# A wave's attention moved behind its casts, wider fillers, and scores of two pairs in one stretch, in a fused attention and MLP kernel

## Chip, cores and metric

The kernel runs on one core of a Trainium2 chip. The metric is the device time of one execution in microseconds. Before the change it is 228.59 us (median of three executions, 228.53 to 228.61). An execution over 1.5% longer than the fastest of its kernel counts as slow. Ratios here use the other, fast, executions alone; the medians given beside them take in all executions of a run. The word "wave" below means 128 positions of each of four batches (512 rows); there are six waves, and in each wave the eight heads are taken as four pairs.

## The reference

```python
def _attn_ref(q, k, v, lam):           # blocks of 64, state carried on
    for b in range(nb):
        intra = (qb @ kb.T) * Dmask            # decay lam**(i-j), causal
        intra = intra @ vb
        inter = (qb * lam_pow) @ kv_state
        out[:, :, sl] = intra + inter
        kv_state = lam_block * kv_state + (kb * rev_pow).T @ vb
def _moe_ref(x, w_in, w_out):          # x: 3072 x 512, d_ff 2048
    h = x @ w_in
    return (h * sigmoid(1.702 * h)) @ w_out
```

The output of the attention, 3072 rows by 512, is the input of the MLP. The kernel uses blocks of 128, and works in bf16 with sums in fp32.

## The kernel before

Every pair p of a wave w passes through these steps. `S` is the scores, `sm` their masking on VectorE, `KV` the new state, `C` the output of the attention. All PSUM tiles below are one bank each: one for transposes, two for scores, one for KV, one for C, three for the MLP.

```python
def cast_k(w, p): ...   # VectorE from wave 2 on: bf16, scaled by the decay; waits for k's DMA
def cast_q(w, p): ...   # the same for q; from wave 2 on followed by a DMA transpose on the sync queue
def step_s(w, p):
    s2 = [ps.tile([P, B, P], f32, tag="s", bufs=2, name="ps_s") for _ in range(2)]
    for b in range(B):
        for h in range(2):               # 64 rows of the array for each head: half-array matmuls
            hs = slice(64 * h, 64 * h + 64)
            nc.tensor.matmul(s2[h][:, b, :], kq[hs, 0, b, :], kq[hs, 1, b, :], start=True, stop=True)
    for h in range(2):
        nc.vector.scalar_tensor_tensor(sm, s2[h], inv_pow[...], mask..., op0=MUL, op1=MUL)
def step_kv(w, p):
    ps_kv = ps.tile([P, B, P], f32, tag="kv", name="ps_kv")     # 4 matmuls, then VectorE adds to kv_sb
def step_c(w, p):
    ps_o = ps.tile([P, B, P], f32, tag="o", name="ps_o")        # 12 matmuls, then ScalarE copies to xT
```

The order of the program is fixed by hand. `main` lists the MLP as items of four matmuls with 512 columns (35 items in waves 0 and 1, about 32 later); `side` puts the attention of the next wave, its casts and its loads between them. `n` is the index of a wave's first item, `e` that behind its last.

```python
for p in range(NP):
    side += [(n + 1 + 2.0 * p, (do_cast, w + 1, p))]
    if w == 1 and p < 2:
        side += [(n + 1 + 2.0 * p, (load, 2, [p + 2]))]
side += [(e - 18 + 2.1 * i, s) for i, s in enumerate(attn_steps(w + 1))]   # S+KV of pair p, then C of pair p-1
```

## Time and profile before

| | before |
|---|---|
| time, median of 3 | 228.59 us |
| time and span of the profiled execution | 226.78 us, 225.1 us |
| PE busy | 211.1 us (94%) |
| PE idle, 73.0 to 77.7 us | 3.95 of 4.7 us |
| one steady wave (wave 2's MLP to wave 3's) | 32.95 us |

The reader should note the second row now. The execution that left the trace was 1.8 us faster than the median. The prediction takes no account of this difference, and that is where it fails.

In a timeline, the first number is the start in us, the second the length; `x8` merges eight instructions, and brackets give how long the engine was idle before and who released it. The lines of the trace that carry the argument stand in the prediction.

### The profile page before, as it was taken

What the parts mean: (1) busy time and instruction counts of PE and PEld (TensorE: products, weight loads), DVE (VectorE), ACT (ScalarE), POOL (GpSimd) and SP (SyncE); (2) the same over time, 40 slices, a digit from 0 to 9 for tenths busy, and PEclk for the clock granted to TensorE, in tenths of its full rate; (3) what the DMA queues carried; (4) which work ended last, traced back from release to release, by engine and by line L of the source; (5) the groups of instructions that cost most, each with busy time, mean ns of one, the idle gap of its engine ahead of it and who ended that gap; (6) DMA issues with size and microseconds to landing.
All of it is one profiled execution on the core that took longest, in us unless ns stands there. A gap on an engine that the chain in (4) does not pass through costs nothing.

```text
span 225.1 us, 3897 instructions
## 1 busy us (share of the span) xinstructions
PE 211.1 (94%) x1514; PEld 112.9 (50%) x1514; DVE 89.8 (40%) x193; ACT 89.7 (40%) x160; POOL 31.8 (14%) x65
## 2 busy tenths in 40 slices
PE   7677999999999299999999999999999999999994
PEld 7565344466444145544455544455544555444454
DVE  0756000189623836280466180665270534100121
ACT  5665863265566011256511266411176321376100
POOL 7117900324021111200111000121000000000000
PEclk9999999999999889999999999999999999999999
DMA  6999999999999998949997159995173011200112
GB/s 129 221 200 219 201 192 205 217 213 275 201 218 197 202 227 191 257 107 159 227 221 177 47 136 191 200 225 142 47 162 71 3 47 47 96 0 0 43 50 96
DMA packets 101590, 34.08 MB, mean 151 GB/s; under 512 B 93636, under 2 KB 98628, under 8 KB 101572
## 3 DMA queue, kind: packets, MB, share of 16 engines
q1 hardware_dynamic: 97204, 29.90, 61.4%
q0 software_dynamic: 4224, 3.93, 11.0%
q8 instruction: 12, 0.20, 0.4%
q14 instruction: 6, 0.05, 0.1%
q10 hardware_dynamic: 144, 0.00, 0.0%
HBM read 27.27 MB, written 6.29 MB: 149 GB/s over the span
## 4 chain that ended last, share of the span: by engine, by line
PE 82%; SPq 6%; DVE 5%; DMA 4%; issue 1%; ACT 1%; DVEq 0%; ACTq 0%
PE ps_h L269 35%; PE ps_out L294 35%; SPq L89 6%; PE ps_o L256 4%; DVE sm L222 3%; PE ps_s L219 2%; PE ps_kv L232 2%; DMA vf<-in_v_dram 2%; PE ps_o L254 2%; PE ps_out L281 2%; DMA qf<-in_q_dram 1%; ACT g_sb L272 1%; DVE kv_151 L239 0%; DVE kv_153 L239 0%; DVE kv_152 L239 0%
## 5 line engine op out<-in xcount | busy, mean ns | idle before, releaser
L272 ACT ACTIVATE g_sb<-ps_h 128x512 bf16<-128x512 f32 x96 | 56.9, 597 | 36.8 <-PE ps_h L269 36.5
L294 PEld LDWEIGHTS <-g_sb 128*128 128x128 bf16 x368 | 34.7, 99 | 37.2 <-issue 1.6
L222 DVE SCALAR_TENSOR_TENSOR sm<-ps_s,inv_pow,mask 128x512 bf16<-128x512 f32 x48 | 33.8, 746 | 31.7 <-PE ps_s L219 31.5
L298 DVE COPY o_sb<-ps_out 128x512 f32<-128x512 f32 x21 | 14.5, 691 | 77.8 <-PE ps_out L294 77.7
L259 ACT CAST xT<-ps_o 128x512 bf16<-128x512 f32 x24 | 14.0, 584 | 64.6 <-PE ps_o L256 64.6
L294 PE MATMUL ps_out<-w_out_165,g_sb 128*128 128x512 bf16 x92 | 24.2, 390 | 0.0
L294 PE MATMUL ps_out<-w_out_166,g_sb 128*128 128x512 bf16 x92 | 23.6, 383 | 0.0
L294 PE MATMUL ps_out<-w_out_167,g_sb 128*128 128x512 bf16 x92 | 23.5, 379 | 0.0
L294 PE MATMUL ps_out<-w_out_164,g_sb 128*128 128x512 bf16 x92 | 23.3, 379 | 0.0
L269 PE MATMUL ps_h<-xT,w_in_163 128*128 128x512 bf16 x96 | 22.4, 379 | 0.0
L269 PE MATMUL ps_h<-xT,w_in_162 128*128 128x512 bf16 x96 | 21.7, 379 | 0.0
L269 PE MATMUL ps_h<-xT,w_in_161 128*128 128x512 bf16 x96 | 21.7, 379 | 0.0
L171 DVE TENSOR_SCALAR kqs<-kf,k_pow 128x256 bf16<-128x256 f32 x40 | 12.7, 348 | 14.8 <-DMA kf<-in_k_dram 9.3
L269 PEld LDWEIGHTS <-w_in_162 128*128 128x128 bf16 x96 | 9.4, 98 | 11.3
L269 PEld LDWEIGHTS <-w_in_161 128*128 128x128 bf16 x96 | 9.4, 98 | 11.3
L269 PEld LDWEIGHTS <-w_in_163 128*128 128x128 bf16 x96 | 9.2, 98 | 10.5
L269 PE MATMUL ps_h<-xT,w_in_160 128*128 128x512 bf16 x48 | 12.0, 379 | 0.7 <-ACT g_sb L272 0.7
L171 DVE TENSOR_SCALAR kqs<-qf,q_pow 128x256 bf16<-128x256 f32 x33 | 10.5, 348 | 3.6 <-DMA qf<-in_q_dram 3.6
L269 PE MATMUL ps_h<-xT,w_in_159 128*128 128x512 bf16 x48 | 11.7, 379 | 0.0
L307 PE MATMUL ps_warm<-ident 128*128 128x128 bf16 x106 | 9.3, 252 | 1.5 <-POOL ident masks.py:199 1.5
L219 PE MATMUL ps_s<-kqT 64*128 64x128 bf16 x128 | 6.6, 219 | 3.4 <-DVE sm L222 3.4
L219 PEld LDWEIGHTS <-kqT 64*128 64x128 bf16 x128 | 3.8, 94 | 10.2 <-issue 7.7
(132 smaller groups left out, 184.5 us busy)
## 6 DMA issues: line engine op xcount, KB each, us to landing
kf<-in_k_dram SPq DMA_DIRECT2D x48, 128.0 KB, 3.6
qf<-in_q_dram SPq DMA_DIRECT2D x48, 128.0 KB, 3.7
vf<-in_v_dram SPq DMA_DIRECT2D x48, 128.0 KB, 3.6
out_dram<-o_sb SPq DMA_DIRECT2D x23, 256.0 KB, 2.4
w_first<-in_moe_w_in_dram SPq DMA_DIRECT2D x1, 512.0 KB, 4.4
w_in_161<-in_moe_w_in_dram POOLq DMA_DIRECT2D x1, 512.0 KB, 6.5
w_in_162<-in_moe_w_in_dram POOLq DMA_DIRECT2D x1, 512.0 KB, 6.8
w_in_163<-in_moe_w_in_dram POOLq DMA_DIRECT2D x1, 512.0 KB, 8.6
```

Source lines behind the costliest of these rows:

```text
L89: nc.sync.dma_start(out=x[:, :, h, :], in_=src[:, 2 * p + h, w * P : (w + 1) * P, :].rearrange("b s d -> s b d"))
L171: eng.tensor_scalar(x[:, i, :, h, :], f[:, :, h, :], scalar1=pw[:, hd : hd + 1], scalar2=None, op0=MUL)
L219: nc.tensor.matmul(s2[h][:, b, :], kq[hs, 0, b, :], kq[hs, 1, b, :], start=True, stop=True)
L222: nc.vector.scalar_tensor_tensor(sm, s2[h], inv_pow[:, 2 * p + h : 2 * p + h + 1], mask.to_broadcast([P, B, P]), op0=MUL, op1=MUL)
L232: nc.tensor.matmul(ps_kv[:, b, :], ks[:, b, :], vt[:, b, 0:3:2, :], start=True, stop=True)
L256: nc.tensor.matmul(ps_o[:, b, :], vt[:, b, h : h + 2, :].rearrange("p c d -> p (c d)"), masked[w, p, h][:, b, :], start=(not w and h == 0) ...
L259: nc.scalar.copy(x, ps_o.rearrange("p b s -> p (b s)"))
L269: nc.tensor.matmul(h_ps[fc], w_in_sb[j][:, kc, i * P : (i + 1) * P], xT[w, kc], start=(kc == 0), stop=(kc == KC - 1))
L272: nc.scalar.activation(g_of[w][:, fc, :], h_ps.pop(fc), GELU)
L294: nc.tensor.matmul(ps_out, g_of[w][:, fc, g * P : (g + 1) * P], w_out_sb[j][:, fc % CW, :], start=(fc == 0), stop=(fc == FFC - 1))
L298: (nc.scalar.copy if w == 0 and g % 2 else nc.vector.tensor_copy)(o, ps_out)
L307: nc.tensor.matmul(warm_ps[:, 0, :], ident, ident, start=True, stop=True)
```

## The change

The masking of wave 2's scores stands behind casts that wait for DMA, and the next scores need the banks that it empties. The change moves wave 2's attention four items later and so lets PE do MLP work first. From wave 2 on, the scores of two pairs follow each other (one entry into the half array in place of two), for which the score banks become four, in one ring with the transposes and, in waves 0 and 1, KV. From wave 2 on KV shares the bank of C. C goes ahead of KV. Fillers that keep PE's clock up in the start-up get 512 columns, four times as wide.

```diff
-        ps_t = ps.tile([P, 2, B, P], bf16, tag="t", name="ps_t")
+        ps_t = ps.tile([P, 2, B, P], bf16, tag="s", bufs=4, name="ps_t")
+    def step_s2(w, p):
+        step_s(w, p)
+        step_s(w, p + 1)
-        s2 = [ps.tile([P, B, P], f32, tag="s", bufs=2, name="ps_s") for _ in range(2)]
+        s2 = [ps.tile([P, B, P], f32, tag="s", bufs=4, name="ps_s") for _ in range(2)]
-            ps_kv = ps.tile([P, B, P], f32, tag="kv", name="ps_kv")
+            ps_kv = ps.tile([P, B, P], f32, name="ps_kv", **(dict(tag="s", bufs=4) if w < 2 else dict(tag="o")))
...
-            nc.tensor.matmul(warm_ps[:, 0, :], ident, ident, start=True, stop=True)
+            nc.tensor.matmul(warm_ps, ident, ident.rearrange("p (o s) -> p o s", o=1).to_broadcast([P, B, P]),
+                             start=True, stop=True)
...
+        if w == 2:
+            at = (0, 1.7, 3.2, 4.8, 6.3, 7.2, 9, 10.4, 12, 13.5)
+        else:
+            at = (0, 2, 4, 6.5, 8.5, 10, 12, 14, 16.5, 18.5)
+        steps = [(f, w, p) for q in (0, 2) for f, p in ((step_s2, q), (step_c, q), (step_kv, q), (step_c, q + 1),
+                                                       (step_kv, q + 1))]
+        return [(i - (14 if w == 2 else 20), x) for i, x in zip(at, steps)]
...   (start-up: keep_warm(40) -> keep_warm(10), 8 and 10 -> 2, C ahead of KV, last KV of waves 0 and 1 later)
-                    side += [(e - 18 + 2.1 * i, s) for i, s in enumerate(attn_steps(w + 1))]
+                    side += [(e + i, s) for i, s in attn_steps(w + 1)]
```

## The prediction

> **What bounds the kernel now.** I read the page first, then the stages, then the order of time around the one bad stage. The page's summary of the engines says that TensorE (PE) is busy 94% of the 225.1 us span, and its row of 40 slices shows where the rest is:
>
> ```profile
> PE   7677999999999299999999999999999999999994
> ...
> PEclk9999999999999889999999999999999999999999
> ...
> DMA  6999999999999998949997159995173011200112
> ```
>
> The reader is to see three things. The first four slices (to about 22 us) are start-up. One slice in the middle (number 14, 73 to 79 us) is nearly empty, and the granted clock drops in it. DMA is full from the start until about there and loose afterwards. The busy time by stage puts numbers on it (columns: stretch and its length in us, then busy us of PE, PEld, DVE, ACT and POOL with instruction counts, granted clock, DMA share, GB/s):
>
> ```profile
> 58.50:73.00 14.50, 14.25 (x78) 6.37 (x75) 4.93 (x14) 9.92 (x17) 1.84 (x3) 1.00 1.04 203
> 73.00:77.70 4.70, 0.75 (x10) 0.43 (x10) 3.64 (x9) 0.00 (x0) 0.61 (x1) 0.93 1.09 213
> 77.70:96.20 18.50, 18.50 (x136) 9.95 (x137) 8.77 (x15) 2.34 (x4) 2.45 (x4) 0.92 0.93 215
> 96.20:129.20 33.00, 33.00 (x226) 16.70 (x225) 16.16 (x36) 11.89 (x20) 2.45 (x4) 1.00 0.82 160
> ```
>
> From 96.2 us on a wave is pure PE: 33 us of 33. So there only PE work can be saved. From 73.0 to 77.7 PE does 0.75 us of work in 4.7. The timeline of that stretch names the cause:
>
> ```profile
> 69.83 0.40 PE L219 MATMUL ps_s<-kqT 64*128 64x128 bf16 x8
> ...
> 74.87 0.35 DVE L171 TENSOR_SCALAR kqs<-qf,q_pow 128x256 bf16<-128x256 f32 x1 [0.20 <-DMA qf<-in_q_dram]
> 75.25 1.41 DVE L222 SCALAR_TENSOR_TENSOR sm<-ps_s,inv_pow,mask 128x512 bf16<-128x512 f32 x2
> 76.05 0.21 PE L219 MATMUL ps_s<-kqT 64*128 64x128 bf16 x1 [2.91 <-DVE sm L222]
> ...
> 77.69 0.58 PE L232 MATMUL ps_kv<-v_sb_144,kqs 128*128 128x128 bf16 x4 [0.59 <-DVE kv_155 L239]
> ...
> 78.07 1.91 PE L294 MATMUL ps_out<-w_out_165,g_sb 128*128 128x512 bf16 x4
> ```
>
> The scores of wave 2, pair 0, are done at 70.2 us. Their masking (sm) starts only at 75.25, because all of wave 2's casts stand ahead of it in VectorE's program, and the last ones wait for q's DMA. The two score banks stay full, so the scores of pair 1 hold PE up. After the gap the clock is down: the eight MLP matmuls from 78.07 to 80.8 take 2.9 us, where eight take 1.73 elsewhere.
>
> **What the Trainium skill says.** "TensorE: Matmul & The Clock Gate", Engine queue depths, calls VectorE a strict FIFO; the masking of finished scores behind a waiting cast agrees. The same page, HAM oscillation, says an idle gap over some 3.4 us lowers the clock; here the waits of 2.9, 0.45 and 0.6 us between 73.2 and 77.7 gave 0.92 to 0.93. "TensorEngine Tiling (Array Packing)", Key Properties, says that changing the tiling mode drains PE. I work this out from the trace: the last MLP matmul before a score stretch ends at 83.39 (four at 215.7 ns from 82.52), scores start at 83.48, and the next full-array matmul at 83.81. Eight score matmuls, two at a time, need about 0.22 us of array time, and took 0.42; so about 0.2 us per stretch is entering and leaving.
>
> **The change, part by part.**
>
> *Start-up.* 40 fillers of 128 columns took 4.25 us (106 ns each, half rate); 10 of 512 are the same columns, so the same time. Later groups go from 8 or 10 small ones (0.45 to 0.56 us) to 2 large ones (about 0.43), and 12 ahead of the first MLP matmuls vanish; KV of the last two pairs also moves out of the way. I estimate 0.3 us at the first MLP matmul and up to 0.7 us more at the first gelus (the ACT copies of KV, 0.76 us, leave their path). I count **0** of it in the total: DMA runs at 190 to 240 GB/s in every stage up to 77.7 us, the sync queue issues without a pause from 35.8 to 76.5 us, and what it loads sets the end of wave 2's casts (75.2 us) whatever PE does earlier. PE only arrives earlier and waits longer.
>
> *Wave 1.* The one ring of four score banks takes A, S, S, KV per pair, just what the separate banks 1+2+1 allowed: 0.
>
> *Wave 2.* The first scores move from 18 to 14 items before the end of wave 1's MLP list. An item is four 512-column matmuls, 0.863 us. In the new order (read from the built program) PE does 2 more mlp1 items and 2 mlp2 items first, then all 16 scores of pairs 0 and 1 into four free banks, then 2 items, then C of pair 0. Without an upstream gain the scores start at 69.83 + 3.45 = 73.28, and the two items end at 73.28 + 0.64 + 1.73 = 75.65. C of pair 0 needs sm, which still ends at 76.66 (75.25 + 1.41, DMA-gated). In wave 1 C ends 0.60 us after its last sm (57.70 to 58.30), so C0 ends at 77.26: about 1 us of waiting in place of 4 us, and no drop of the clock.
>
> From there I add durations of this trace: item 0.863, C 0.667 (12 matmuls at 55.6 ns), KV 0.22, double scores 0.64. KV and C now share the one "o" bank. The KV update on VectorE starts 0.52 us after KV's first matmul (48.73 to 49.25) and takes 0.97, and PE resumes about 0.13 later (77.54 to 77.69): 1.62 us from KV's start to the next C. Where only one item stands between (0.22 + 0.86 = 1.08), that is a stall of **0.54 us**.
> - items 23, 24 to 78.99; KV0; item 25 to 80.07; stall to 80.61; C1 to 81.28
> - items 26, 27 to 83.00; KV1; item 28 to 84.09; scores of pairs 2, 3 to 84.73
> - sm of pair 2 ends at 84.18 + 0.43 + 1.41 = 86.02 to 86.03; item 29 ends at 85.6, so C2 ends at 86.63 and not 86.27: a stall of 0.36
> - items 30, 31 to 88.36; KV2; item 32 to 89.44; stall to 89.98; C3 to 90.65
> - items 33, 34 to 92.37; KV3; mlp1 of wave 2 starts at **92.6**.
>
> Before, it starts at 96.21. Gain **3.6 us**, after 1.44 us of new stalls.
>
> *Waves 3 to 5.* Two score stretches fewer per wave, each worth about 0.2 us: 0.4 a wave, **1.2 us**. Here two or three items stand between KV and C, and 1.73 us of items between the second score pair and C, so I expect no stall. Scores need pair 1's transpose earlier (12 items, 10.4 us after the wave's first mlp1). In the trace transposes start some 2.1 us after that point, 1.3 us apart, and land 3.3 us after issue: about 7 us. It fits.
>
> *The end* (last mlp2 pieces and the output) is untouched. Sum: 3.6 + 1.2 = 4.8 us; 228.6 - 4.8 = **223.7 us**.
>
> **The rivals.**
>
> *The shared bank bites harder.* KV and C alternate in one bank, evacuated by two engines. If each of the handovers in wave 2 costs a further 0.3 us, or some appear in waves 3 to 5, the time is 225 to 226. For it: VectorE is strictly in order, so a copy or an sm ahead of the KV update lengthens it. Against: after 78 us VectorE is busy less than half of the time (8.77 of 18.50).
>
> *The stalls are smaller than I add.* If VectorE picks KV up sooner, up to 1.4 us come back: 222.3. My latencies come from rows in which VectorE was free, so I hold most of this unlikely.
>
> *The start-up gain reaches the end.* It would add 0.5 to 1 us: 222.9. This needs DMA to come earlier, and nothing in its order changes.
>
> *DMA takes over.* If the transfers of wave 2 end at 75.2 and those of wave 3 matter next, wave 3 could stall, since PE arrives 3.6 us earlier. Its loads are issued from 76.6 to 91.3 us and take 3.6 us to land, its casts now start at about 93.5 us with pair 0, and pair 3's cast at 98.7: it fits, with little to spare for pair 0's output and transposes. Failing here would cost 1 to 2 us: 225.
>
> **Range and chances.** The gain in wave 2 is sure in sign: a 4.7 us hole is mostly filled with work that is there. Its size hangs on DMA's gate (half a us either way) and the stalls (0 to 2.5 us). The score saving is small but repeated. So 222.0 to 225.5 holds it 8 times in 10. The border of 2% is 224.02, only 0.3 us above my value: faster 0.62, within 2% 0.37, slower 0.01.
>
> **What would show each step.** Right: the slice at 73 to 79 us fills, with a granted clock near 1 in it; sm of wave 2's first pairs still starts near 75.2 us; first mlp1 of wave 2 near 92.6; steady waves of about 32.5 us (before: 32.9); short PE waits on the KV update before C of pairs 1 and 3 in wave 2, about 0.5 us each. Wrong: sm of wave 2 starting a us or more earlier or later (DMA moved with PE), PE waits ahead of C in waves 3 to 5, PE waiting on transposes, or a steady wave that is no shorter, which would mean that entering and leaving the half array is not what the 0.2 us were. Start-up may show mlp1 starting 0.3 us sooner, and wave 1 giving it back.

## The result, and the profile after

After: **221.61 us** (median of 4 executions, 221.56 to 221.85). Before, with one more execution: 228.56 us. The ratio is 0.9706, 95% interval 0.9683 to 0.9729. A ratio is the mean time of one kernel's fast executions over that of the other's from the same rounds, so it isn't quite the ratio of the medians. The result lies 2.1 us under my 223.7 and 0.4 under the end of my range.

The spans of the two profiled executions tell another story: 225.1 and 220.1 us, 5.0 us apart, where I had 4.8. The page of after has no row for the clock, as it never dropped. Its row of PE in 40 slices has lost the empty slice:

```profile
PE   7786999998999799999999999999999999999994
```

The stages of after, with the columns of the table in the prediction:

```profile
73.00:77.70 4.70, 3.35 (x37) 1.99 (x36) 2.90 (x6) 0.00 (x0) 0.62 (x1) 1.00 1.00 153
77.70:96.20 18.50, 17.90 (x133) 9.41 (x132) 11.65 (x23) 4.14 (x7) 2.47 (x4) 1.00 1.05 231
96.20:129.20 33.00, 33.00 (x228) 17.04 (x227) 17.78 (x43) 12.37 (x21) 2.46 (x4) 1.00 0.75 164
```

PE works 3.35 us of 4.7 where it worked 0.75, at a clock of 1.00. The timeline of after in wave 2:

```profile
72.90 0.62 PE L224 MATMUL ps_s<-kqT 64*128 64x128 bf16 x16
...
75.51 2.73 DVE L227 SCALAR_TENSOR_TENSOR sm<-ps_s,inv_pow,mask 128x512 bf16<-128x512 f32 x4
...
76.31 0.22 PE L257 MATMUL ps_o<-sm,v_sb_143 128*128 128x128 bf16 x1 [0.90 <-DVE sm L227]
...
76.97 0.22 PE L257 MATMUL ps_o<-sm,v_sb_143 128*128 128x128 bf16 x1 [0.44 <-DVE sm L227]
...
80.71 0.23 PE L255 MATMUL ps_o<-kqT,kv_152 128*128 128x128 bf16 x1 [0.20 <-DVE kv_155 L244]
...
86.19 0.22 PE L257 MATMUL ps_o<-sm,v_sb_145 128*128 128x128 bf16 x1 [0.19 <-DVE sm L227]
...
92.56 1.89 PE L270 MATMUL ps_h<-xT,w_in_159 128*128 128x512 bf16 x8
```

All 16 score matmuls of two pairs go out at once. The masking starts at 75.51, still behind the casts; PE waits 0.9 and 0.44 us in C of pair 0. Before C of pair 1 there is the wait for the KV update in the shared bank. The MLP of wave 2 starts at 92.56 us; the prediction has 92.6. The next wave's starts at 125.08, so a steady wave takes 32.52; the prediction has 32.5. These steps hold, and the total does not. The experiments had to find where two more microseconds come from.

### The profile page after: what moved, and what is told of

The parts are those of the page before. It is cut to its first block, busy times and chain, and to the rows that moved or that the text cites. A ratio compares the mean times of both kernels' runs of the same rounds, so it can differ in the third digit from the quotient of the medians.

```text
span 220.1 us, 3721 instructions
## 1 busy us (share of the span) xinstructions
PE 208.8 (95%) x1430; PEld 107.5 (49%) x1430; DVE 90.2 (41%) x193; ACT 89.3 (41%) x160; POOL 31.9 (14%) x65
## 4 chain that ended last, share of the span: by engine, by line
PE 58%; DVE 0%; issue 0%
PE ps_h L270 25%; PE ps_out L295 24%; PE ps_o L257 3%; PE ps_out L282 2%; PE ps_s L224 2%; PE ps_o L255 1%; PE ps_kv L237 1%; DVE o_sb L284 0%
## 5 line engine op out<-in xcount | busy, mean ns | idle before, releaser
L295 PEld LDWEIGHTS <-g_sb 128*128 128x128 bf16 x368 | 34.2, 98 | 36.2
L227 DVE SCALAR_TENSOR_TENSOR sm<-ps_s,inv_pow,mask 128x512 bf16<-128x512 f32 x48 | 33.1, 744 | 18.8 <-PE ps_s L224 18.6
L295 PE MATMUL ps_out<-w_out_167,g_sb 128*128 128x512 bf16 x92 | 23.5, 379 | 0.0
L295 PE MATMUL ps_out<-w_out_166,g_sb 128*128 128x512 bf16 x92 | 23.3, 380 | 0.0
L295 PE MATMUL ps_out<-w_out_164,g_sb 128*128 128x512 bf16 x92 | 23.3, 379 | 0.0
L295 PE MATMUL ps_out<-w_out_165,g_sb 128*128 128x512 bf16 x92 | 23.3, 379 | 0.0
L270 PEld LDWEIGHTS <-w_in_161 128*128 128x128 bf16 x96 | 9.3, 98 | 11.5 <-DMA w_in_161<-in_moe_w_in_dram 0.4
L270 PEld LDWEIGHTS <-w_in_162 128*128 128x128 bf16 x96 | 9.3, 98 | 11.4 <-DMA w_in_162<-in_moe_w_in_dram 0.4
L270 PEld LDWEIGHTS <-w_in_163 128*128 128x128 bf16 x96 | 9.0, 98 | 10.2
L308 PE MATMUL ps_warm<-ident 128*128 128x512 bf16 x22 | 8.1, 497 | 1.5 <-POOL ident masks.py:199 1.5
L237 PEld LDWEIGHTS <-kqs 128*128 128x128 bf16 x80 | 5.9, 98 | 4.4 <-issue 0.8
L270 PEld LDWEIGHTS <-w_in_160 128*128 128x128 bf16 x48 | 4.6, 97 | 6.0 <-DMA w_in_160<-in_moe_w_in_dram 1.0
```

The costliest lines, as they stand in the source:

```text
L227: nc.vector.scalar_tensor_tensor(sm, s2[h], inv_pow[:, 2 * p + h : 2 * p + h + 1], mask.to_broadcast([P, B, P]), op0=MUL, op1=MUL)
L237: nc.tensor.matmul(ps_kv[:, b, :], ks[:, b, :], vt[:, b, 0:3:2, :], start=True, stop=True)
L270: nc.tensor.matmul(h_ps[fc], w_in_sb[j][:, kc, i * P : (i + 1) * P], xT[w, kc], start=(kc == 0), stop=(kc == KC - 1))
L295: nc.tensor.matmul(ps_out, g_of[w][:, fc, g * P : (g + 1) * P], w_out_sb[j][:, fc % CW, :], start=(fc == 0), stop=(fc == FFC - 1))
L308: nc.tensor.matmul(warm_ps, ident, ident.rearrange("p (o s) -> p o s", o=1).to_broadcast([P, B, P]), start=True, stop=True)
```

## The experiments

There were sixteen runs, in four calls; the runs of a call were on one chip. Some repeat a kernel under a second label, to have it on another chip. All gave correct results. "Before" is run again beside them in each call, and its median moved between 227.7 and 229.3 us from chip to chip, so I compare ratios across calls and times within one.

### The kernel before, again (a_before_again)

No edit.

> The kernel before, unchanged, for the clock and span of each timed execution. The profiled execution of before took 226.78 us at a mean clock of 0.992, the timed ones 228.6. Theory clock: the hole at 73 to 78 us makes the granted clock drop for a longer time in most executions, so a run at 228.6 has a mean clock near 0.984 (1.8 us lost at half rate is 3.6 us of half rate, 0.016/2 of 226 us more), and span and time differ by 1.7 us in every run. Rival: the clock is the same 0.992 in the slow and the fast executions, and the extra 1.8 us are waiting (DMA).

Measured: 229.04 us (228.41 to 230.16, 14 executions), ratio 1.0006. Time and span differ by 1.7 to 1.9 us in every execution, nearly as expected. Neither theory alone held. The mean granted clock comes in steps: about 0.992, 0.985, 0.977. A step of 0.0075 over 226 us is 3.4 us at half rate (0.0075 x 2 x 226). "TensorE: Matmul & The Clock Gate" of the Trainium skill, What's actually happening, has an activity window of 3413 ns, and the steps agree with it: one, two or three windows at half rate. Over the fast executions of before of all four calls, 37 with one window took 228.06 us on average, 36 with two took 229.33, and 4 with three 229.55. The calls mix these differently, so the cost is better read within a call: 228.37 and 229.50 in the first, 228.32 and 229.24 in the second. So a second window goes with about 1 us more. Most executions of after have none (12 of 16). The mean does not say where a window lies, and not every one lies at the hole: the traces of b and g below have one in the start-up, from 18.2 and 19.9 us.

The execution that I had read had a single window, and it was also the fastest that I had seen by then (3 of the 84 in the four calls were shorter); even one-window executions are 1.3 us longer on average.

The trace of this run is a typical one, with span 227.4 and clock 0.985. The start of wave 2's MLP in the trace of before, on which the prediction rests, and then from this run the row of the clock of the page, the stage behind the hole, and the lines of the timeline that differ:

```profile
96.21 1.03 PE L269 MATMUL ps_h<-xT,w_in_159 128*128 128x512 bf16 x4
```

```profile
PEclk9999999999999769999999999999999999999999
...
77.70:96.20 18.50, 17.79 (x133) 9.90 (x133) 10.04 (x18) 1.75 (x3) 2.56 (x5) 0.83 0.97 214
...
26.23 10.53 PE L269 MATMUL ps_h<-xT,w_in 128*128 128x512 bf16 x48 [1.25 <-DMA w_in<-in_moe_w_in_dram]
...
71.16 0.40 PE L219 MATMUL ps_s<-kqT 64*128 64x128 bf16 x8
...
76.55 1.41 DVE L222 SCALAR_TENSOR_TENSOR sm<-ps_s,inv_pow,mask 128x512 bf16<-128x512 f32 x2
...
77.36 0.26 PE L219 MATMUL ps_s<-kqT 64*128 64x128 bf16 x1 [2.88 <-DVE sm L222]
...
79.37 3.62 PE L294 MATMUL ps_out<-w_out,g_sb 128*128 128x512 bf16 x8
...
98.55 1.67 PE L269 MATMUL ps_h<-xT,w_in 128*128 128x512 bf16 x7
```

The masking starts 1.3 us later than in the trace that I had (76.55 for 75.25), all eight MLP matmuls behind the hole and more run at half rate, and the MLP of wave 2 starts at 98.55 for 96.21: 2.34 us, which is the whole difference of the spans (2.3). The hole itself is no longer: PE waits 2.9, 0.4 and 0.4 us in it, where before had 2.9, 0.45 and 0.6. PE comes to it 1.3 us late (first scores at 71.16 for 69.83), after a wait of 1.25 us for a w_in transfer at 25 us that the trace of before does not have. As the scores of pair 1 wait for the masking, PE would have been held to the same time without that wait too. **By the start of wave 2's MLP this execution has lost 2.3 us more than the one I priced**: some 1.3 as its transfers land later, from the start-up on, and the rest, 1.0, by the clock. The clock after the hole, in two stretches, for before and then for this run (the column before the last two):

```profile
77.10:80.40 3.30, 2.71 (x10) 1.29 (x11) 2.71 (x5) 0.00 (x0) 0.00 (x0) 0.50 0.94 202
80.60:83.80 3.20, 3.20 (x31) 1.74 (x29) 0.69 (x1) 0.58 (x1) 0.61 (x1) 1.00 1.03 221
```

```profile
77.10:80.40 3.30, 2.25 (x15) 1.26 (x15) 3.25 (x7) 0.00 (x0) 0.61 (x1) 0.50 0.87 180
80.60:83.80 3.20, 3.20 (x16) 1.75 (x15) 0.56 (x2) 0.00 (x0) 0.00 (x0) 0.50 1.03 224
```

The drop begins within 0.1 us of the same time in both, though the hole ends 1.3 us later here; it lasts one window in before and two here.

### Fillers in the hole (b_before_filled)

```diff
+        if (w, p) == (2, 1):
+            fill_ps = ps.tile([P, B, P], f32, tag="mm", bufs=3, name="ps_fill")
+            for _ in range(12):
+                nc.tensor.matmul(fill_ps, ident, ident...to_broadcast([P, B, P]), start=True, stop=True)
         step_s(w, p)
```

> Before, with 12 filler matmuls of 512 columns (2.6 us of PE) in the hole, ahead of the scores of wave 2, pair 1; nothing else changes, and the waiting of PE for sm stays. Theory clock: the clock stays at 1.0, the slow matmuls behind the hole go: 1.1 us less than the profiled 226.8, so about 225.6 timed, 3 us under before. Rival (the extra time of the timed executions is waiting): 228.6 - 1.1 = 227.4, with a mean clock near 1.0 in both.

Measured: 227.52 us, ratio 0.9927 (0.9905 to 0.995), 1.7 us under before. As a time this is the rival's 227.4; but before took 229.3 on this chip, and the saving of 1.7 lies between the theory's 3 and the rival's 1.2. In 12 of 22 executions the clock was 0.999 or more, and their mean is 227.2; in the others it still dropped. The trace of b, one of those, has a drop behind the waits that are left (0.8, 0.45 and 0.6 us) and another in the start-up, where the fillers of this run can do nothing. In the same call's before, the 14 executions with one window have a mean of 228.4 and the 17 with two 229.5. So two windows cost before about 2.3 us, and keeping PE busy in the hole takes much of that away without any change to the waiting; that both lie at the hole is what the trace of a shows, and not known for the other executions. The rest of my 225.6 may be missing because DMA was late here too (sm at 77.04 in the one trace).

### Wave 2 late, alone (c_before_w2_late, o_late_again)

```diff
-side += [(e - 18 + 2.1 * i, s) for i, s in enumerate(attn_steps(w + 1))]
+side += [(e - 14 + 1.85 * i if w == 1 else e - 18 + 2.1 * i, s) for i, s in enumerate(attn_steps(w + 1))]
```

> Before, with only wave 2's attention four items later (single scores, two score banks, old start-up). If the hole is what the change removes: some 3.0 us of the wait and all of the clock's loss (1.1 + 1.8 us) go: 222.7 us, clock 1.0. If the four banks are what matters in wave 2, the scores of pair 1 still wait for sm of pair 0 (until about 76.1 us) and the gain is below 3 us: 226.

> Before with wave 2 four items later only, on the same chip as after: double scores (1.2 us in waves 3 to 5 and 0.4 in wave 2) and the new start-up (0 to 1.1) are what it lacks, less the new waits for the shared bank (0.7): 1.5 us above after.

Measured: 223.94 us, ratio 0.9755 (0.972 to 0.979), and on another chip 225.20 us, ratio 0.9795 (0.9746 to 0.9844). One changed expression gives 4.7 to 5.6 of the 7 us, with two score banks. But on the chip of the second run it lies 3.0 us above after (222.24 there), not 1.5. Its trace shows waits of 0.56, 0.45 and 0.59 us in a row around the scores of pair 1, followed by a drop of the clock from 79.7 us; it also has late transfers (sm at 76.84, where c has 75.46). In two of its six executions the clock is 0.992, and a third is as slow at 1.0. So a row of short waits was once followed by a lost window; what the rest of the 3.0 us is stays open.

### The late start undone (p_after_w2_early)

```diff
-        return [(i - (14 if w == 2 else 20), x) for i, x in zip(at, steps)]
+        return [(i - (18 if w == 2 else 20), x) for i, x in zip(at, steps)]
```

> After, with only the delay of wave 2 undone (its scores 18 items before the end of wave 1's list, as in before; four banks, double scores and new start-up stay). Theory: sm still starts at 75.3 us behind the casts, PE runs out of work two items after the double scores (near 72 us) and waits for more than 3 us, and the clock drops: 3.5 us of lost order and 1 to 2 us of clock above after, 226 to 227 us. Rival: four score banks take the wait away by themselves: within 1 us of after.

Measured: 225.33 us, ratio 0.9814 (0.9765 to 0.9862), where after in the same call has 0.9663: 3.5 us. That is the size that I expected of the order of the work alone, but it holds some loss of the clock too: the three executions at 0.999 or more have a mean of 224.5, 2.7 above the fast executions of after, and the two fast ones with a window lost 226.4. The clock stayed up in these three against what I had expected. Its trace (a slow execution) has the wait of before again, 3.8 us ahead of the masked scores, plus 1.4 us for a transpose that isn't there yet:

```profile
77.06 0.22 PE L257 MATMUL ps_o<-sm,v_sb 128*128 128x128 bf16 x1 [3.80 <-DVE sm L227]
```

So four banks do not take the wait away; the late start does.

### The start-up (d_after_old_start, g_after_small_fill, h_before_big_fill)

d puts the old start-up code into after. g only turns each filler of after into four small ones. h only turns the fillers of before into large ones:

```diff
-        for _ in range(n):
-            nc.tensor.matmul(warm_ps[:, 0, :], ident, ident, start=True, stop=True)
+        for _ in range(n // 4):
+            nc.tensor.matmul(warm_ps, ident, ident...to_broadcast([P, B, P]), start=True, stop=True)
```

> After, with the start-up of before (small fillers, KV ahead of C, old places of the last KV of wave 0). My prediction counted 0 for the start-up: within 0.3 us of after (221.6). Rival: the start-up gain reaches the end: 222.3 to 222.6.

> After, but each filler of 512 columns is again four of 128 (the same columns and the same places; 66 more matmuls and 66 more weight loads in PE's program ahead of the first MLP matmul). Theory instruction fetch: a 16 KB packet of PE's program comes at 12.8 us in every run with small fillers, SP's issue of a v load next to it takes 1.8 us in place of 0.55, and all later transfers come later; then this run has it too, w_first is issued near 14.7 us and not 13.4, and the time is 1 to 1.5 us above after. Rival: the order of C and KV makes the difference between the start-ups; then this run equals after within 0.3 us and w_first is issued near 13.4.

> Before, with fillers of 512 columns (10, 2, 2, 2, 1 for 40, 8, 10, 8, 4). Theory instruction fetch: the packet at 12.8 us moves to about 18 us, SP does not stop, w_first is issued near 13.4, sm of wave 2 starts about 1 us sooner, and the time falls 1 us under before. Rival: 0.

After run d I compared the sync queue in all traces. The kernel before and then h (the same loads in the same order, only the fillers differ), both from 12 us on:

```profile
12.28 2.40 SPq L89 DMA_DIRECT2D vf<-in_v_dram  x2
14.73 0.55 SPq L75 DMA_DIRECT2D w_first<-in_moe_w_in_dram  x1
```

```profile
12.15 1.13 SPq L89 DMA_DIRECT2D vf<-in_v_dram  x2
13.33 0.54 SPq L75 DMA_DIRECT2D w_first<-in_moe_w_in_dram  x1
```

The queue loses 1.2 us at the v loads, with no wait that the profile names. The view of DMA traffic from 12 to 14 us names a candidate in before, and h has no such line:

```profile
q8 instruction: 1, 0.02, 4.1%
```

It is one packet of 16 KB, 1.3 us long, at 12.76 us: a fetch of the program. In all seven traces with small fillers the first such packet comes at 11.8 to 12.9 us, and the v loads take 1.9 to 2.5 us in place of 1.1; in all traces with large fillers it comes at 17.7 to 18.8 us, when (in those that I looked at) that queue has nothing to issue. I take it for PE's program, since it moves with the number of PE's instructions alone; the profile doesn't say whose it is. "Runtime: NRT & Kernel Launch", Instruction fetch mechanics, speaks of blocks of 16 KiB whose cost is "mostly hidden". The size agrees; if the packet is what stopped the queue, it was not hidden here.

What it is worth is less sure. h: 227.85 us, ratio 0.9951 (0.9931 to 0.9972), a gain of 1.1 us, and its masking starts at 74.78. g: the fetch and the stop came as expected (w_first at 14.41), yet 222.9 us and a ratio of 0.9726 (0.9678 to 0.9774) can't be told from after's 0.9717 on the same chip. d: 223.25 us, ratio 0.9742 (0.9709 to 0.9774). That is 0.6 to 1.8 us above the three ratios of after, none of which is from d's call, and d also undoes the new order of C and KV. The start of the masking in traces where it stands behind the casts is 76.2 us on average over seven with small fillers (75.25 to 77.04) and 75.55 over eight with large ones (74.78 to 76.25); the two ranges overlap. So large fillers are worth 1.1 us in before, and in after something between nothing and 1 us. My 0 was too low in before's terms, and the way that the traces suggest is not the one I had in mind: DMA comes earlier, though its order is the same. That the fetch is what delays it is not shown apart from the fillers, which also let PE start its MLP 0.9 us sooner in h.

### Single scores (i_after_again, e_after_single_scores)

e puts the second score pair of each stretch one item later:

```diff
+            if x[0] is step_s:
+                out.append((o + 1, (step_s, w, x[2] + 1)))
```

> After, unchanged, on the chip of the next three. Its four executions so far had spans of 219.9 to 220.1 at clock 1.0. If the chip and not the start-up made the run with the old start-up longer (221.3 to 222.1), after shows 221 to 222 here as well; if the start-up did, 220.

> After, with the scores of the second pair of each stretch one item later, so eight stretches more of half array in waves 2 to 5. My prediction put 0.2 us on each: 1.6 us above after (1.2 of it in waves 3 to 5, a steady wave of 32.9 in place of 32.5). Rival: entering and leaving costs nothing and the stretch of 0.42 us is its work: within 0.2 us of after.

Measured: after 222.00 us, ratio 0.9717 (0.9667 to 0.9767); with single scores 223.43, ratio 0.9768 (0.9728 to 0.9808). The intervals overlap, but the traces agree in each of the two steady waves that I compared. One steady wave of e, and the same of after, by the stretch view:

```profile
93.03:125.97 32.94, 32.62 (x223) 16.65 (x225) 17.28 (x38) 11.90 (x20) 3.07 (x5) 1.00 0.79 184
```

```profile
92.56:125.08 32.52, 32.52 (x228) 16.83 (x226) 17.25 (x38) 11.90 (x20) 3.09 (x5) 1.00 0.80 185
```

Each wave is 0.42 us longer, 0.21 for each stretch more, with the same number of score matmuls. The prediction's "about 0.2 us per stretch" is measured here. "TensorEngine Tiling (Array Packing)", Key Properties, says that a mode switch drains PE; it gives no duration, and this is one for entering and leaving together.

### The waits that the change leaves (f_after_kv_ring, j_after_cast_behind, k_both, n_both_again)

f gives KV the score ring in all waves. j puts the casts of pair 3 of wave 2, and the loads behind them, after the first double scores in the program. k and n are both, and C and KV of pair 2 later.

```diff
f:  -ps_kv = ps.tile(..., **(dict(tag="s", bufs=4) if w < 2 else dict(tag="o")))
    +ps_kv = ps.tile(..., tag="s", bufs=4)
j:  -side += [(n + 1 + 2.0 * p, (do_cast, w + 1, p))]
    +side += [(e - 13.99 if (w, p) == (1, NP - 1) else n + 1 + 2.0 * p, (do_cast, w + 1, p))]
    -side += [(n + 8, (load, w + 2, range(NP)))]
    +side += [(e - 13.95 if w == 1 else n + 8, (load, w + 2, range(NP)))]
k:  both, and 9, 10.4 -> 9.7, 10.9 in the list of wave 2
```

> After, with KV of waves 2 on in the ring of four score banks in place of the bank of C. Theory shared bank: in the trace of after PE waits 0.4 us ahead of C of pairs 1 and 3 in wave 2 for the KV update; both go, 0.7 us in all, waves 3 to 5 stay at 32.5: ratio to before 0.003 lower than after's 0.9717. Rival: VectorE is what holds PE there, and the wait moves to the next score stretch or to C of pair 2: no change.

> After, with the casts of wave 2's pair 3 (and the loads of wave 3 that follow them on the sync queue) put behind the scores of pairs 0 and 1 in the program, so that sm no longer stands behind a cast that waits for q. Theory: sm starts at about 73.4 us, PE's wait of 1.3 us ahead of and in C of pair 0 goes: 1.3 us less than after, and the time no longer follows DMA (spans of the executions within 0.5 us). Rival: the gate moves to the transpose of pair 3 and PE waits as long ahead of the scores of pairs 2 and 3: no change.

> Both of these, and C of wave 2's pair 2 one item later. If the three waits of wave 2 add up: 1.3 + 0.7 + 0.3 = 2.3 us less than after, about 219.7 us, ratio to before 0.962.

> The version with both changes (casts of pair 3 behind the scores, KV in the score ring) on the same chip as after: 2.3 us less than after by the waits that it takes away (1.3, 0.7, 0.3).

> After, unchanged, as the reference of the next three on one chip. On the chips so far its ratio to before was 0.9706 and 0.9717, with before between 227.7 and 229.3: 221 to 222 us here, spans near 220.

Measured, with before at 227.72 us on this chip: f 220.98 (ratio 0.9721), j 220.31 (0.9695), k **219.65** (0.966, 0.9618 to 0.9702). Against after on one chip: m, after, 222.24 us (ratio 0.9663, 0.9611 to 0.9714) and n 220.57 (0.96, 0.9563 to 0.9637). The best version is 1.4 us faster than after (the difference of the ratios times 229), with overlapping intervals, and clearly faster than before.

In f's trace the waits for the KV update are gone and only those for sm (1.4 us) stay. In j's the masking starts at 73.59 and the wait of C for pair 0 is gone, and those for KV (0.4 us) stay. Each theory held in its trace; f's ratio does not show it. After is not in that call and before was faster on that chip, which may be why. In k's trace PE waits for nothing from 66 to 94 us. After and then k, by the stretch view:

```profile
66.00:94.00 28.00, 26.05 (x192) 13.44 (x190) 15.37 (x30) 6.84 (x12) 3.08 (x5) 1.00 1.08 212
```

```profile
66.00:94.00 28.00, 28.00 (x204) 14.81 (x203) 17.94 (x40) 8.68 (x15) 3.42 (x5) 1.00 1.04 194
```

All 1.95 us that PE was idle in after are filled, and k's MLP of wave 2 starts at 89.50 us, 3.06 earlier (its next wave takes 32.82 us, so 0.3 of that goes back). The timed executions of k and n gain less than the traces (span 217.4 and 217.5 there, mostly 218 to 219 in the others). What the others lost I have no trace of. The rival of j, that PE would wait as long for the transpose of pair 3, does not show in its trace. But one part of its theory failed: the spans were to lie within 0.5 us of each other, and they differ by 1.4. n is 1.4 us under after where 2.3 were expected.

### The sum of the parts (l_late_big_fill)

Wave 2 late and large fillers, both edits from above, in before.

> Before, with wave 2 four items later and the fillers of 512 columns; single scores and separate banks stay. If the parts add up: 0.9755 for the first and 0.9951 for the second give 0.9707, and after (0.9717) would owe nothing more to double scores, which cannot be, as single scores cost after 1.2 us; so I expect a loss of the sum: the later start takes up DMA's variation, and this run lies near 0.975, 0.5 to 1.2 us above after. If it lies at 0.971, start-up and double scores do not add.

Measured: 224.23 us, ratio 0.9855 (0.9806 to 0.9904) with f at 0.9721 on the same chip: 3.0 us of difference where traces give 1.7 (221.3 and 219.6). I had expected about 0.975: the parts do not add here, and the late start alone (0.9755 and 0.9795 on other chips) did better. The waits of its trace are 1.15, 0.44 and 0.6 us in wave 2, and three of its six executions have a clock near 0.99; where in them the clock dropped is not known. Why it is not faster than c and o stays open.

## Why the prediction was wrong, point by point

- **The cause of the hole, and its removal.** Right. Undoing the late start alone costs 3.5 us; the late start alone brings 4.7 to 5.6.
- **"mlp1 of wave 2 starts at 92.6".** Right: 92.56. Inside it, sm ended later than I had it and C of pair 0 came 0.2 us late, while the waits for the bank were 0.4 in place of 0.54; that these evened out to 0.04 us is luck.
- **"Waves 3 to 5: 0.4 a wave, 1.2 us".** Right: 32.52 for 32.95, and 0.42 by experiment e.
- **"I count 0 of it" for the start-up.** Wrong for before (1.1 us), open for after. That nothing in DMA's order changes was right, but it did not rule out what I took it to: the masking starts 0.6 us earlier on average in traces with large fillers, in ranges that overlap.
- **"Before, it starts at 96.21 ... 228.6 - 4.8".** This is the step that failed, and that put the result out of the range. The 96.21 is from an execution of 226.78 us and the 228.6 from others; I took a saving from the one off the other. Taken off its own execution, 226.8 - 4.8 = 222.0, 0.4 from the result. In the typical execution of run a the MLP of wave 2 starts at 98.55, as its transfers land 1.3 us later and the clock is down for two windows and not one (1.0 us). Against after's trace that is 6.0 + 1.2 = 7.2 us; 7.0 was measured. Not all of the 6.0 is the late start's doing: 1.0 of it is that the masking starts at 76.55 in a and at 75.51 in after. Whether the new fillers or chance brought after's transfers earlier is not shown.
- The loss of clock that I read off eight matmuls (2.9 us for 1.73; they end at 81.0 and not at the 80.8 that I wrote) was a sample of something that varies by execution: one, two or three windows in before.

What stays open: how the rest divides between DMA's lateness and the clock in executions without a trace, why the start-up's gain shows in before and hardly in after, and what the timed executions of the best version lose against its traces.

## What to carry to other kernels

Before pricing a hole from a trace, compare the time of the traced execution with the median: if they differ, the hole may be what differs, and the saving has to be taken off the same execution. The hole in PE's work here cost more than its length, as the clock was down for 3.4 or 6.8 us behind it; such a hole is best filled with work that is already there, by moving the dependent step later in a queue that runs in order. Then look for what stands ahead of it in that queue: here moving a cast behind the masking, and giving two tiles two banks, took away the waits that were left.

## What the Trainium skill lacked or had wrong

- "TensorE: Matmul & The Clock Gate", HAM oscillation, speaks of idle gaps of more than about 3.4 us. Here no single gap was that long in before (2.9, 0.45 and 0.6 us), and in run o a drop followed gaps of only 0.56, 0.45 and 0.59 us. The page does tell elsewhere of a kernel with short, frequent idles, but gives no length for them. The same kernel lost one to three windows of 3.4 us in an execution, the second going with about 1 us.
- "TensorEngine Tiling (Array Packing)", Key Properties, gives no duration for the drain at a mode switch: 0.21 us for entering and leaving a stretch of 64-row matmuls.
- "Runtime: NRT & Kernel Launch", Instruction fetch mechanics, calls the fetch of a 16 KiB block mostly hidden: here such a packet took 1.3 us amid small transfers, the sync queue stood still for 1.2 us beside it, and the fillers that moved it brought 1.1 us in before. That the fetch was the cause is inferred.
- No page says that the transfers of one kernel land more than a microsecond apart in different executions: the masking behind the last q started at 75.25 us in one trace of before and at 76.55 in another.
